# Keys and values of a linear attention as seven block products, and a softmax's divisions moved to the output's stage

## The chip, the cores and the metric

The kernel runs on one core of one Trainium2 chip. The metric is the device time of one execution in microseconds (us). TensorE (PE) multiplies, VectorE (DVE), ScalarE (ACT) and GpSimd (POOL) do elementwise work, and SyncE (SP) issues nearly every DMA. Each engine works through its own list of instructions in order; semaphores connect the lists.

## The reference

Two attention blocks read the same input of 2048 tokens by 1024 features and are mixed by a gate per token. Both have 32 heads of 32 features.

```python
g = _sigmoid((x * gate_w).sum(-1, keepdims=True))
# A: linear attention
phi = lambda t: jnp.where(t > 0, t + 1, jnp.exp(t)) + 1e-6
pq, pk = phi(q), phi(k)
kv = jnp.einsum("bhsd,bhse->bhde", pk, v)
z = jnp.einsum("bhsd->bhd", pk)
o = jnp.einsum("bhqd,bhde->bhqe", pq, kv) / (jnp.einsum("bhqd,bhd->bhq", pq, z)[..., None] + 1e-6)
# B: softmax attention
p = _softmax(jnp.einsum("bhqd,bhkd->bhqk", q, k) * (Dh ** -0.5), axis=-1)
o = jnp.einsum("bhqk,bhkd->bhqd", p, v)
# each o goes through its own wo
return g * a + (1 - g) * b
```

## The kernel before

Every float32 operand of a projection is split into a high part (a rounding copy on ACT) and a low part (the rest, a subtraction on DVE or GpSimd). One product of a 128 x 128 tile with a 128 x 512 tile is then three matmuls of 512 columns (high-high, high-low, low-high), by the helper `three` (L146 to L148) or written out (L407 to L409, L446 to L448).

The work runs in these stages:

- **Queries and keys of B, and half of its values.** Queries and keys are computed as seven block products in place of eight (Winograd's form of Strassen's product): `v_next` and `v_sums` make the four sums `t1` to `t4` of the input's blocks, `pair_ops` makes those of the weights on GpSimd, and `product` (L404) multiplies. `spill` (L329) writes the split input to DRAM (`xs`), one store per product.
- **The stream `lin`** (function `linear`, L707) then works through units of one token tile of 128 tokens and one chunk of 512 output columns, 24 matmuls each: 16 units `v` (rest of B's values), 64 units `kv` (four chunks of 256 key and 256 value columns), 32 units `q` and 32 units `o` (A's queries, and its product with `kv` and the output weights). A `kv` unit ends in `phi` on ACT (L564 to L566), one DVE instruction (L778), a running sum of the keys on GpSimd (L783, `zsum`) and eight small products in `keys` (L584). The next chunk's weights are loaded and split while the last unit of a chunk runs (`load_w`, `split_w`, L547 and L549).
- **Mixes.** During `q` and `o` units, `load_mix` (L632) brings a quarter of A's output weights into a tile, and `mix` (L649) multiplies `kv` into it. The planner lets a mix stand 8 us of its own time after the load.
- **The streams `max` and `head`** do the softmax attention of the 32 heads beside `lin`. For every head there are 64 score steps in each: `max` multiplies queries by keys (L887) and DVE takes the row maxima (L892); `head` multiplies the other way round (L1038) and ACT takes the exponential (L1042). Every four steps make one probability tile of 2048 columns, in a ring of seven. Its columns are summed over the tiles, 1536 of them on GpSimd (L1085, L1089) and 512 on DVE (`own`, L1098), and groups of five or six tiles are multiplied by the values (L1136). `finish` (L931) adds the sums over the partitions (L940); DVE then inverts them (L947), multiplies (L950), and SP stores the head's output to `oB_d`.
- **The stream `out`** multiplies B's output by its output weights, after `load_o`, `split_o` (L1191) and `gate`, and mixes in A's.

The order on PE, DVE, ACT, POOL and SP is written by a planner at the end of the kernel. It has its own clock `T` per engine and its own costs, and takes at each step the stream that can start and is furthest behind; work on DVE that may wait lies in `later` (`defer`, `fill`). The order is fixed when the program is built. `RATE_Q` and `rates` say how many `lin` matmuls stand beside one score step.

Of the kernel before, what the change touches and what calls it, by code (L numbers as in the profile page):

```python
# [18 lines left out]
P = 128  # L19
# [12 lines left out]
AHEAD = {"head": 0, "max": 6, "lin": 9, "out": 0}  # L32
# [4 lines left out]
SLACK = 0.4  # L37
WARM = 8
WO_STEP = 4
LATE = 1.0  # L40
MANUAL = {ET.PE, ET.DVE, ET.Activation, ET.SP, ET.Pool}
NMID = 14
# [3 lines left out]
def kernel(  # L46
# [53 lines left out]
    ra_d = [dram.tile([P, D], F32, name=f"ra{t}") for t in range(NT)]  # L100

# [13 lines left out]
    mh = sb.tile([NT, P], F32R, name="mh")  # L115
    ml = sb.tile([NT, P], F32R, name="ml")
# [36 lines left out]

    def use(eng, cost, *after):

        T[eng] = max(T[eng], *after, 0.0) + cost
        return T[eng] + LATENCY[eng]
# [51 lines left out]
    held = [False] * 8  # L209
    RING = [0, 1, 2, 3, 5, 6]  # L210

    def bank_at():

        times = [ended(readers[b], free[b]) for b in RING if not held[b]]
        return min((at for at in times if at is not None), default=None)

    def take():

        idle = [b for b in RING if not held[b]]
# [5 lines left out]
        held[b] = True  # L225
        return b
# [28 lines left out]
    def load_cols(w, cols, k, n):  # L255

        raw = raw_tile(n)
# [71 lines left out]
    def spill(js):  # L329

        for half in range(2):
            for jj in (1, 0):
                for i in range(TPC):
                    for p in range(2):
                        src = big[XO[PLACE[jj][half]][p]].rearrange("p (k c) -> p k c", c=C)
                        t = js[jj] * TPC + i
                        nc.sync.dma_start(xs[p][t][:, half * HK:(half + 1) * HK, :],
                                          f32(src[:, :, i * P:(i + 1) * P]))
                        yield
# [92 lines left out]
    for np_, js in enumerate(PAIRS):  # L432
        final = np_ + 1 == len(PAIRS)
        side = spill(js)
        todo = iter(())
        base = used
        for pos, k in enumerate(KORDER):
# [3 lines left out]
            for t in range(2 * TPC):  # L441
# [6 lines left out]
                nc.tensor.matmul(ps, stat[1], w[0], start=False, stop=(pos == NK - 1))  # L448
            if half:
                v_sums(i)  # L450
        used += NK
# [8 lines left out]
        for g in range(NK):  # L460
            nxt = pair_ops(g + 1) if g + 1 < NK else None
            for q, name in enumerate(PRODUCTS):
# [37 lines left out]
                next(side, None)  # L500
# [3 lines left out]
        for _ in side:  # L504
            pass
# [6 lines left out]
    chunks = [("v", c) for c in range(1, NQC)] + [("kv", c) for c in range(D // HC)]  # L512
    chunks += [(kind, c) for kind in ("q", "o") for c in range(NQC)]
    units = [(i, (t + NT // 2) % NT if chunks[i][0] == "v" else t) for i in range(len(chunks)) for t in range(NT)]
# [19 lines left out]
    def load_w(kind, c, k, n):  # L534
        if kind == "v":
            raw = load_cols(b_wqkv, vcols(c), k, n)
        elif kind == "kv":
            raw = load_cols(a_wqkv, [(D + c * HC, HC), (2 * D + c * HC, HC)], k, n)
# [11 lines left out]

    def load_xp(n):
# [5 lines left out]
        xp_ready[n % 2] = T["pe"] + 4.0  # L557
        for p, src in enumerate(oA_d if kind == "o" else xs):
# [13 lines left out]
    def keys(n, c, t, pk, va, todo):  # L572
# [3 lines left out]
        def products(b, at):  # L576
# [11 lines left out]
            def total(_):  # L588
                part = pb.rearrange("p (k d) -> p k d", d=DH)
                if t == 0:  # L590
# [10 lines left out]
    def keys_now(until):  # L601
# [4 lines left out]
        if ready:  # L606
            b = take()
# [19 lines left out]
    def load_mix():  # L627
# [5 lines left out]
        mix_here.append((a, c, T["pe"] + 8.0))  # L633
# [36 lines left out]
    z_end = [0.0, 0.0]  # L670

    def keysum(c):

        yield lambda: both(bank_at(), z_end[c % 2])
        b = take()
# [8 lines left out]
    def queries(n, c, t, pq, todo):  # L684
# [4 lines left out]
        b = take()  # L689
# [16 lines left out]

    def linear():  # L707
        extra = iter(())
        coming_w = deque()
        for n, (i, t) in enumerate(units):  # L710
            kind, c = chunks[i]
            pos = n % NT
            here_ = n < NT // 2
            follow = chunks[i + 1] if i + 1 < len(chunks) else None
            xp = xp_t[n % 2]
            yield bank_at
# [6 lines left out]
            if kind in ("q", "o") and c == 0 and t in (2, 8, NT - 2):  # L723
                yield lambda: None if mix_here else 0.0
                if t < NT - 2:
                    load_mix()
            if n < 2:
                load_head(n)
                load_v(n)
            for k in range(NK):  # L730
# [17 lines left out]
                if k == NK - 1:  # L748
# [660 lines left out]
```

## Time and profile before

| what | value |
|---|---|
| median of three runs | 2873.7 us (2872.09 to 2874.22) |
| the profiled execution | 2873.77 us, span of its instructions 2872.0 us |
| granted TensorE clock, mean | 0.996 |
| busy: VectorE | 2239.1 us |
| busy: ScalarE | 1617.8 us |
| busy: GpSimd | 1854.1 us |
| moved by DMA | 400.57 MB, mean 139 GB/s |

By the first and last starts of the lines, the stages lie in the span as follows: seven-product stage 0 to 399 us, units `v` to 504, `kv` to 1720, `q` to 2160, `o` to about 2690, output to the end. Busy time of PE includes waits inside its pipeline, so a stage is read by how many matmuls it holds per microsecond as well as by its busy share.

### The profile page before, as it was taken

The page shows a single profiled execution, that of the slowest core. Times are in us where ns is not written, and L with a number is a line of the kernel's source. Part 1 is how long each engine was busy: PE and PEld are TensorE (multiplying, and loading weights), DVE is VectorE, ACT ScalarE, POOL GpSimd, SP SyncE. Part 2 cuts the span into 40 slices and gives each one's busy share as a digit, 9 for nine tenths or more (in the row PEclk, how much of TensorE's full clock was granted, in tenths as well). Part 3 has the DMA queues.
Part 4 walks back from the last instruction along what each step waited for, and adds up shares of the span by engine and source line. Part 5 has one row for each costly group of instructions (what it writes and reads, how often), then busy time and mean ns, then how long its engine had stood idle before and what let it go on. Part 6 is the DMA issues. An engine that isn't in the chain of part 4 may idle for free.

```text
span 2872.0 us, 44436 instructions
## 1 busy us (share of the span) xinstructions
PE 2846.1 (99%) x15744; PEld 2036.8 (71%) x15744; DVE 2239.1 (78%) x3775; ACT 1617.8 (56%) x3007; POOL 1854.1 (65%) x646
## 2 busy tenths in 40 slices
PE   9999999999999999999999999899999999999999
PEld 8888888666666666666666666566766666666687
DVE  7667656788888888888888888778888888886643
ACT  5334321666666667666666666566666656656421
POOL 1212220778898889888988887578778877885000
PEclk9999999999999999999999999999999999999999
DMA  5956764332333233333332235554465344524663
GB/s 179 284 174 212 247 201 152 121 93 92 108 89 92 89 101 110 90 92 92 120 93 90 76 120 168 173 185 145 135 195 167 114 137 133 144 88 143 213 219 105
DMA packets 302498, 400.57 MB, mean 139 GB/s; under 512 B 92682, under 2 KB 185354, under 8 KB 299146
## 3 DMA queue, kind: packets, MB, share of 16 engines
q1 hardware_dynamic: 302276, 397.73, 44.8%
q8 instruction: 124, 2.03, 0.3%
q14 instruction: 98, 0.80, 0.1%
HBM read 287.57 MB, written 108.79 MB: 138 GB/s over the span
## 4 chain that ended last, share of the span: by engine, by line
PE 96%; DMA 2%; DVE 1%; ACT 0%; issue 0%; SPq 0%; ACTq 0%; DVEq 0%
PE bank L1038 16%; PE bank L887 16%; PE bank L1136 15%; PE bank L146 11%; PE bank L148 11%; PE bank L147 11%; PE bank L407 4%; PE bank L409 4%; PE bank L408 4%; PE bank L446 1%; PE bank L940 1%; PE bank L447 1%; PE bank L448 1%; DMA big<-xs 1%; PE bank L693 0%; PE bank L584 0%
## 5 line engine op out<-in xcount | busy, mean ns | idle before, releaser
L1089 POOL TENSOR_TENSOR big<-big,big 128x1536 f32<-128x1536 f32 (+1 forms) x434 | 1556.4, 3586 | 188.9 <-ACT big L1042 166.7
L892 DVE TENSOR_REDUCE mx<-bank 128x1 f32<-128x512 f32 x2048 | 1311.4, 681 | 319.6 <-PE bank L887 315.1
L1042 ACT ACTIVATE big<-bank 128x512 f32<-128x512 f32 x2048 | 1180.6, 601 | 524.8 <-PE bank L1038 455.6
L1038 PE MATMUL bank<-big,big 128*128 128x512 f32 x2048 | 810.7, 397 | 2.7 <-ACT big L1042 2.6
L887 PE MATMUL bank<-big,big 128*128 128x512 f32 x2048 | 803.6, 392 | 3.2 <-ACT mid L342 2.9
L146 PE MATMUL bank<-big,big 128*128 128x512 f32 x1408 | 552.7, 393 | 5.7 <-DMA big<-xs 3.4
L148 PE MATMUL bank<-big,big 128*128 128x512 f32 x1408 | 550.9, 391 | 1.0 <-DMA big<-oA 0.6
L147 PE MATMUL bank<-big,big 128*128 128x512 f32 x1408 | 550.6, 391 | 0.0
L1038 PEld LDWEIGHTS bank<-big,big 128*128 128x128 f32 x2048 | 384.6, 188 | 159.7 <-issue 62.0
L1136 PE MATMUL bank<-big,mid 128*32 128x512 f32 x4096 | 461.1, 595 | 0.0
L887 PEld LDWEIGHTS bank<-big,big 128*128 128x128 f32 x2048 | 385.4, 188 | 87.4 <-ACT big L1042 3.7
L1136 PEld LDWEIGHTS bank<-big,mid 128*32 128x32 f32 x4096 | 127.9, 110 | 266.2 <-issue 266.2
L146 PEld LDWEIGHTS bank<-big,big 128*128 128x128 f32 x1408 | 264.6, 188 | 71.0 <-ACT big L1042 4.3
L148 PEld LDWEIGHTS bank<-big,big 128*128 128x128 f32 x1408 | 264.8, 188 | 57.6 <-DMA big<-oA 1.0
L147 PEld LDWEIGHTS bank<-big,big 128*128 128x128 f32 x1408 | 264.5, 188 | 55.3
L1098 DVE TENSOR_TENSOR bank<-bank,big 128x512 f32<-128x512 f32 (+1 forms) x434 | 280.6, 647 | 7.8 <-ACT big L1042 6.1
L1085 POOL TENSOR_TENSOR big<-big,big 128x1536 f32<-128x1536 f32 (+1 forms) x31 | 111.6, 3601 | 253.0 <-ACT big L1042 135.5
L253 DVE TENSOR_TENSOR big<-mid,big 128x512 fp32r<-128x512 f32 x216 | 153.0, 732 | 80.5 <-ACT big L252 80.5
L386 POOL TENSOR_TENSOR mid<-mid,mid 128x512 f32<-128x512 f32 x16 | 20.6, 1291 | 276.7 <-DVE big L253 250.6
L252 ACT CAST big<-mid 128x512 fp32r<-128x512 f32 x216 | 130.2, 624 | 95.8 <-POOL mid L387 54.0
L407 PE MATMUL bank<-big,big 128*128 128x512 f32 x448 | 174.3, 389 | 0.0
L408 PE MATMUL bank<-big,big 128*128 128x512 f32 x448 | 174.3, 389 | 0.0
(103 smaller groups left out, 1981.9 us busy)
## 6 DMA issues: line engine op xcount, KB each, us to landing
big<-xs SPq DMA_DIRECT2D x208, 512.0 KB
qk<-mid SPq DMA_DIRECT2D x128, 256.0 KB
big<-oA SPq DMA_DIRECT2D x64, 512.0 KB
big<-qk SPq DMA_DIRECT2D x96, 256.0 KB
big<-qk SPq DMA_DIRECT2D x384, 64.0 KB
mid<-in_b_wqkv SPq DMA_DIRECT2D x88, 256.0 KB
xs<-big SPq DMA_DIRECT2D x64, 256.0 KB
oA<-mid SPq DMA_DIRECT2D x64, 256.0 KB
```

The costliest lines, as they stand in the source:

```text
L146: yield nc.tensor.matmul(ps, sh, mh_, start=(kt == 0), stop=False)
L147: yield nc.tensor.matmul(ps, sh, ml_, start=False, stop=False)
L148: yield nc.tensor.matmul(ps, sl, mh_, start=False, stop=(kt == NK - 1))
L407: nc.tensor.matmul(ps, sh, mh_, start=(i == 0), stop=False)
L408: nc.tensor.matmul(ps, sh, ml_, start=False, stop=False)
L887: nc.tensor.matmul(bank[b], q[:, t * P:(t + 1) * P], k[:, j * C:(j + 1) * C], start=True, stop=True)
L892: nc.vector.tensor_reduce(m[:, t, j:j + 1], bank[b], AX.X, ALU.max)
L1038: nc.tensor.matmul(bank[b], k[:, t * P:(t + 1) * P], q[:, j * C:(j + 1) * C], start=True, stop=True)
L1042: nc.scalar.activation(pr_t[i][:, j * C:(j + 1) * C], bank[b], AF.Exp, scale=SCALE)
L1089: nc.gpsimd.tensor_add(lacc[:, :qp], lacc[:, :qp], pr(t)[:, :qp])
L1098: nc.vector.tensor_add(lacc[:, qp:] if t == NT - 1 else l_b[:, :n], l_b[:, :n], src)
L1136: nc.tensor.matmul(av_b[j * DH:(j + 1) * DH, :], v[:, t, :], pr(t)[:, j * C:(j + 1) * C], start=(t == 0), stop=(t == NT - 1))
```

## The change

**Keys and values.** The 64 `kv` units become 112 products of 12 matmuls (L994): two sets of two chunks, eight pairs of token tiles, seven products each. The sums of the input's blocks are those of the first stage; they are stored there (`spill_t`, to `xt_d`) and read back. The sums of A's weights are made on GpSimd (`w_sums`, L604), the first set's during the units `v`, the second's during the products, and stored to `wt_d`. Partial results are copied out by ACT (`copy_u`, L879), some stored to `u_d` and loaded again (`load_u`); a later product starts on a bank into which ACT has copied such a result (L948), or DVE adds it (`add_u`, L886). Outputs go through `kv_out`, a stream of its own, which holds what a `kv` unit held at its end. The low parts of 56 weight tiles are made on GpSimd except those of the first eight, where there were 32 tiles, the first eight on DVE.

**Softmax sums.** For all heads but the last, `finish` copies the sums to SBUF (`l_sb`, L1285) and stores one row of each 32. After 8, 8, 8, 4 and 3 heads a packed tile is loaded, inverted in one DVE instruction (L1296) and stored to `r_d`. In the output's stage `load_r` brings the inverses of a token tile, each repeated over 32 partitions, and `scale_o` multiplies on GpSimd (L1567) ahead of `split_o`. The head's unscaled output is stored as soon as ACT has copied it.

**Planner.** `LATE` is -1.0 in place of 1.0: ahead of a row maximum the planner takes work that may wait only if it ends 1 us before the maximum can start; `own` stands in bunches in the new order, in halves where one follows another. A mix stands 25 us of planned time after its load in place of 8. `kv` has a rate of its own, 1.4, `lin` may run ahead by 40 in place of 9, and ties look at DVE's and ACT's clocks. The weights of the first chunk of `kv` are all loaded three units ahead into eight tiles in place of five.

```diff
-AHEAD = {"head": 0, "max": 6, "lin": 9, "out": 0}
+RATE_KV = 1.4
+AHEAD = {"head": 0, "max": 6, "lin": 40, "kvout": 0, "out": 0}
...
+MIX_LAND = 25.0
-LATE = 1.0
+LATE = -1.0
...
+    PHASES = ((("b11", "x"), ("b21", "x")), (("t2", "t2"),), (("t3", "t1"), ("t4", "x")), (("t1", "t3"), ("b22", "t4")))
...
+        return ([loads],
+                [lambda: add(sub, r11, r11, r12), lambda: add(plus, r12, r22, r12),
+                 lambda: add(sub, r22, r22, r11), lambda: add(sub, r21, r21, r22)],
+                [lambda n=n, r=r: store(n, r) for n, r in (("t1", r11), ("t3", r12), ("t2", r22), ("t4", r21))])
...
-        mix_here.append((a, c, T["pe"] + 8.0))
+        mix_here.append((a, c, T["pe"] + MIX_LAND))
...
+    ORDER = []
+    for m in range(NPAIR + 1):
+        ORDER += [(0, pr, q) for pr, q in ((0, m), (1, m - 1)) if 0 <= q < NPAIR]
+    ORDER += [(1, 0, q) for q in range(NPAIR)]
+    ORDER += [(2, pr, q) for q in range(NPAIR) for pr in range(2)]
+    for m in range(NPAIR + 1):
+        ORDER += [(3, pr, q) for pr, q in ((0, m), (1, m - 1)) if 0 <= q < NPAIR]
...
+        SEED = {(0, 1): (S1, lambda q: q % 4), (1, 0): (S1, lambda q: q % 4), (2, 1): (U2, lambda q: q % 2 * 2),
+                (3, 0): (U2, lambda q: q % 2 * 2), (3, 1): (W5, lambda q: q % 2 * 2)}
...
+                end = use("act", 0.6, free[b], u_at[i])
+                nc.scalar.copy(bank[b], u_tiles[i])
...
+            for k in range(HK):
...
+                for j, (x_, w) in enumerate(((sh, wh), (sh, wl), (sl, wh))):
+                    nc.tensor.matmul(bank[b], x_, w, start=(k == 0 and j == 0 and not seeded),
+                                     stop=(k == HK - 1 and j == 2), skip_group_check=seeded)
...
+                w_step()
+                if pi in last_of:
+                    split_w(None, None, slot, *loaded.popleft(), nc.gpsimd)
...
+            load_x(pi + 4)
...
                 if k == 1 and n + 1 == len(units):
+                    load_r(0, KF)
+                if k == NK - 1 and n + 1 == len(units):
                     split_o(0, slice(0, NK - 1))
-                if k == NK // 2 and n + 1 == len(units) and over["head"]:
-                    split_o(1, slice(0, NK - 1))
...
-        def store(_):
-            nc.vector.tensor_mul(avs, avs, pl)
-            for j in range(NJ):
-                nc.sync.dma_start(oB_d[j * TPC:(j + 1) * TPC, rows, g, :].rearrange("t p c -> p t c"),
-                                  avs[j * DH:(j + 1) * DH, :].rearrange("p (t c) -> p t c", c=P))
...
+        if h < H - 1:
+            need(r_left)
+            end = use("act", 0.5, end)
+            give(b, end)
+            nc.scalar.copy(l_sb, pl)
+            nc.sync.dma_start(l_d[h].rearrange("(j c) -> j c", c=C),
+                              l_sb.rearrange("(j e) c -> j e c", e=DH)[:, 0, :])
...
+                def back(_):
+                    nc.vector.reciprocal(part, part)
+                    nc.sync.dma_start(flat[1], part)
...
+            parts = 2 if after_own[0] and n == C else 1
...
+    def scale_o(n, ks):
+        rows = slice(0, P if ks == KF else LAST.start)
+        part = o_part(n, ks)[rows]
+        r = f32(blocks(xo_t[n % len(xo_t)], 1)[rows, ks])
+        nc.gpsimd.tensor_mul(part, part, r)
```

The planner's order shows three places. The first is PE in the middle of the keys and values. Before (L146 to L148 a `kv` unit, here into bank_244, with L887 and L1038 the two score matmuls):

```order
L148 MATMUL bank_244<-big_224,big_212 128x512
L146 MATMUL bank_244<-big_224,big_212 128x512
L887 MATMUL bank_249<-big_211,big_210 128x512
L147 MATMUL bank_244<-big_224,big_212 128x512
L148 MATMUL bank_244<-big_224,big_212 128x512
L1038 MATMUL bank_243<-big_208,big_209 128x512
L887 MATMUL bank_246<-big_211,big_210 128x512
L1038 MATMUL bank_245<-big_208,big_209 128x512
```

The same place of the changed kernel, where L994 is a product and L1209 and L1377 are the two score matmuls:

```order
L994 MATMUL bank_299<-big_277,big_262 128x512 x2
L1377 MATMUL bank_295<-big_260,big_261 128x512
L994 MATMUL bank_299<-big_277,big_262 128x512
L1209 MATMUL bank_297<-big_261,big_258 128x512
L1377 MATMUL bank_296<-big_260,big_261 128x512
L1209 MATMUL bank_294<-big_261,big_258 128x512
L1377 MATMUL bank_300<-big_260,big_261 128x512
L1209 MATMUL bank_295<-big_261,big_258 128x512
L994 MATMUL bank_299<-big_277,big_262 128x512
L994 MATMUL bank_297<-big_276,big_262 128x512
```

Products and scores lie interleaved as the units and scores did; bank_299 is finished and the next product begins in bank_297. Over the whole of this stage the order holds 1196 steps of each score stream before and 1012 after.

The second place is GpSimd in the same stage. Before (L1085 and L1089 sum probability tiles, L783 sums keys):

```order
L1089 TENSOR_TENSOR big_3757<-big_3757,big_3755 128x1536
L783 TENSOR_TENSOR mid_235<-mid_235,mid_232 128x256
L1089 TENSOR_TENSOR big_3757<-big_3757,big_3749 128x1536
L1089 TENSOR_TENSOR big_3757<-big_3757,big_3750 128x1536
L1089 TENSOR_TENSOR big_3757<-big_3757,big_3751 128x1536
```

After, in the last products of the first set (L1429 sums tiles, L849 sums keys, L640 makes a low part of a weight, and the sums of the second set's weights are L604 rows in between, as `big_3941<-big_3941`):

```order
L1429 TENSOR_TENSOR big_3939<-big_3939,big_3933 128x1536
L604 TENSOR_TENSOR big_3941<-big_3941 128x512
L1429 TENSOR_TENSOR big_3939<-big_3939,big_3934 128x1536
L604 TENSOR_TENSOR big_3941<-big_3941 128x512
L849 TENSOR_TENSOR mid_285<-mid_285,mid_284 128x256
L604 TENSOR_TENSOR big_3941<-big_3941 128x512
L1429 TENSOR_TENSOR big_3939<-big_3939,big_3935 128x1536
L849 TENSOR_TENSOR mid_285<-mid_285,mid_282 128x256
L1429 TENSOR_TENSOR big_3939<-big_3939,big_3936 128x1536
```

Weight sums and key sums now stand between nearly every two tile sums there.

The third place is ACT where the output begins (L252 before and L270 after split; 128x896 is seven eighths of one token tile of B's output, L822 and L1142 copy the last `o` units out, L1216 and L1599 belong to the gate). Before:

```order
L252 CAST big_21242<-mid_233 128x512
L252 CAST big_212<-big_3758 128x896
L252 CAST big_21207<-big_3753 128x896
L822 COPY mid_239<-bank_244 128x512
L1216 ACTIVATE g_sb<-g_sb 128x1
```

After:

```order
L270 CAST big_261<-mid_280 128x512
L270 CAST big_262<-big_3941 128x896
L1142 COPY mid_289<-bank_295 128x512
L270 CAST big_22034<-mid_282 128x512
L270 CAST big_22034<-mid_283 128x512
L270 CAST big_274<-big_3936 128x896
L1599 ACTIVATE g_sb<-g_sb 128x1
```

The second token tile's split stands behind the last `o` unit's copy now, and each of the two has a GpSimd multiplication ahead of it that is not in this list.

More of the change, by code (lines that the diff above doesn't have):

```diff
@@ L209, with bank_at, take @@
     held = [False] * 8
+    whole = [True] * 8
     RING = [0, 1, 2, 3, 5, 6]
-    def bank_at():
-        times = [ended(readers[b], free[b]) for b in RING if not held[b]]
+    def bank_at(seed=False):
+        times = [ended(readers[b], free[b]) for b in RING if not held[b] and (whole[b] or not seed)]
         return min((at for at in times if at is not None), default=None)
-    def take():
-        idle = [b for b in RING if not held[b]]
+    def take(seed=False, part=False, kept=False):
+        idle = [b for b in RING if not held[b] and (whole[b] or not seed)]
         times = {b: ended(readers[b], free[b]) for b in idle}
@@ L225, in take @@
         held[b] = True
+        whole[b] = whole[b] if kept else not part
         return b
@@ L670 @@
     z_end = [0.0, 0.0]
+    z_left = [[] for _ in range(2 * NSET)]
     def keysum(c):
-        yield lambda: both(bank_at(), z_end[c % 2])
-        b = take()
+        z_wait.remove(c)
+        need(z_left[c])
+        b = take(part=True)
         pz = bank[b]
@@ new lines, with u_free, load_u, copy_u @@
+    u_tiles = [mid[i] for i in (8, 9, 10, 14)]
+    u_left = [[] for _ in u_tiles]
+    u_at = [0.0] * len(u_tiles)
+    S1, U2, P7, W5 = range(4)
+    def u_free(i):
+        need(u_left[i])
+        u_left[i].clear()
+        return u_tiles[i]
+    u_what = [None] * len(u_tiles)
+    def load_u(what, pair, i):
+        nc.sync.dma_start(u_free(i), u_d[what][pair])
+        u_what[i] = what, pair
+        u_at[i] = T["pe"] + 7.0
+    def copy_u(i, b, what, pair):
+        u = u_free(i)
+        u_at[i] = use("act", 0.5, T["pe"] + LATENCY["pe"])
+        nc.scalar.copy(u, bank[b])
+        u_what[i] = what, pair
+        if what in (S1, U2, P7):
+            nc.sync.dma_start(u_d[what][pair], u)
+        return u_at[i]
@@ L890, in maxima @@
                 fill(end + LATE)
+                while True:
+                    fit = [it for it in later if it.rank <= 1 and due(it) and it.at <= T["dve"]]
+                    if not fit:
+                        break
+                    run(min(fit, key=lambda it: (it.rank, it.at)))
                 give(b, use("dve", 0.605, end))
@@ L1360 @@
             wait = max(at - T["pe"], 0.0)
-            key = (wait > 0.02, wait if wait > 0.02 else -lag)
+            busy = max(T["dve" if name == "max" else "act"] - T["pe"], 0.0) if name in ("max", "head") else 0.0
+            key = (wait > 0.02, wait + TIE * busy if wait > 0.02 else -lag, wait)
             if best is None or key < best[0]:
```

413 lines of the change are left out of this document (342 added, 71 removed).

## The prediction

> **What bounds the kernel now.** I read the page's head first, then the stretches by stage, then what PE waited for. Head and chain:
>
> ```profile
> span 2872.0 us, 44436 instructions
> PE 2846.1 (99%) x15744; PEld 2036.8 (71%) x15744; DVE 2239.1 (78%) x3775; ACT 1617.8 (56%) x3007; POOL 1854.1 (65%) x646
> PE 96%; DMA 2%; DVE 1%; ACT 0%; issue 0%; SPq 0%; ACTq 0%; DVEq 0%
> ```
>
> The chain that ended last lies on PE for 96% of the span. A busy PE need not be a full one, so I take the stretches by stage (columns: length, busy time and count of PE, weight loads, DVE, ACT, POOL, then granted clock, DMA share, GB/s):
>
> ```profile
> 0.00:399.00 399.00, 397.16 (x1743) 328.98 (x1744) 269.12 (x406) 167.46 (x294) 95.80 (x77) 1.00 0.69 214
> 399.00:504.00 105.00, 105.00 (x465) 86.70 (x464) 59.52 (x88) 13.85 (x24) 0.00 (x0) 1.00 0.59 182
> 504.00:1720.00 1216.00, 1213.06 (x7527) 826.16 (x7527) 1036.18 (x1762) 795.69 (x1535) 1055.44 (x374) 1.00 0.33 98
> 2680.00:2872.00 192.00, 185.84 (x823) 151.26 (x822) 87.25 (x204) 41.09 (x58) 0.00 (x0) 1.00 0.55 179
> ```
>
> The second row holds 512-column matmuls and nearly nothing else: 105.00 / 465 = 0.226 us each. The first gives 0.228. In the third the six matmul streams fill 1213 of 1216 us, while DVE is at 85%, POOL at 87% and ACT at 65%. So PE's matmuls set the time, and a matmul taken away is worth 0.226 to 0.228 us unless something else becomes late. What PE waited for:
>
> ```profile
> PE bank L649 <- DMA big<-in_a_wo: 7.5, 1, 7.5
> PE bank L146 <- DMA big<-xs: 3.4, 2, 2.0
> PE bank L887 <- ACT mid L342: 2.9, 1, 2.9
> PE bank L1038 <- ACT big L1042: 2.6, 1, 2.6
> PE bank L146 <- ACT big L252: 1.9, 1, 1.9
> ```
>
> These five are 18 us. Some cost more than their length:
>
> ```profile
> 506.00:516.00 10.00, 7.06 (x20) 5.55 (x20) 7.34 (x12) 6.29 (x11) 0.00 (x0) 0.66 1.00 258
> 1848.00:1854.00 6.00, 3.96 (x19) 2.99 (x18) 4.58 (x9) 4.40 (x8) 5.84 (x3) 1.00 0.67 236
> 1915.00:1925.00 10.00, 7.39 (x34) 4.23 (x36) 6.23 (x12) 5.43 (x10) 7.28 (x2) 0.83 0.69 244
> 1829.48 3.79 PE bank L649 x32
> 1789.80 1.09 PE bank L649 x32
> 1833.27 3.10 PE bank L1136 x16
> 1790.89 1.85 PE bank L1136 x16
> ```
>
> The first three are short windows around waits of 2.9, 2.0 and 2.6 us: granted clock 0.66, 1.00 and 0.83. The others are rows of the chain: the mix that came after the wait of 7.5 us took 3.79 us, its fellow at 1789 took 1.09, and the attention matmuls behind it 3.10 against 1.85. Here a wait of 2.6 us or more is followed by a stretch at half clock, one of 2.0 us isn't. The Trainium skill (TensorE: Matmul & The Clock Gate, section Why this matters for your kernels) puts the limit at about 3 us of idle time; the rows put it lower. By its limit new waits just under 3 us would cost only themselves and the sum below would be 1 to 2 us less; the measured rows decide.
>
> **The change, part by part.** The sum is made against the profiled execution, 2873.77 us, which is the median (2873.7) but for 0.1.
>
> *Matmuls.* Four chunks of 16 units of 24 matmuls, 1536, become 2 x 8 x 7 products of 12, 1344: 192 fewer. At 0.226 to 0.228 us that is 43.4 to 43.8 us, say **-43.6**. The small products, the transposes, the scores and the attention matmuls keep their counts; the scores that no longer stand beside `kv` stand beside `o`.
>
> *The mix's wait.* A mix stands 25 us behind its load in place of 8. The wait of 7.5 us, the 2.7 us by which that mix was slow (3.79 - 1.09) and 1.25 of the attention rows go: **-11.4**. What could be late next are the `xs` loads behind it (3.4 us, kept in the sum).
>
> *The first `kv` weights.* At 508 us ACT was held up by a late weight and released a bank late, 2.9 us and then a clock of 0.66. All eight weights are loaded earlier now, but DMA's share in that window is 1.00, and the input's and weights' sums now load it more. From -6 to +1; I take **-3**.
>
> *New work on ACT and DVE.*
>
> ```profile
> L1042 ACT ACTIVATE big<-bank 128x512 f32<-128x512 f32 x2048 | 1180.6, 601 | 524.8 <-PE bank L1038 455.6 <-POOL big L1089 3.2 <-issue 2.6
> L342 ACT COPY mid<-bank 128x512 f32<-128x512 f32 x32 | 18.4, 588 | 91.8 <-PE bank L148 87.5 <-PE bank L448 2.1 <-DMA v<-mid 2.1
> L947 DVE RECIPROCAL bank<-bank 128x128 f32<-128x128 f32 x128 | 123.3, 963 | 3.5 <-PE bank L940 0.4
> L950 DVE TENSOR_TENSOR mid<-mid,bank 128x512 f32<-128x512 f32 x31 | 21.3, 686 | 1.0
> L1098 DVE TENSOR_TENSOR bank<-bank,big 128x512 f32<-128x512 f32 x364 | 251.0, 689 | 5.7 <-ACT big L1042 4.5
> L1098 DVE TENSOR_TENSOR bank<-bank,big 128x256 f32<-128x256 f32 x70 | 29.7, 424 | 2.1 <-ACT big L1042 1.7
> L892 DVE TENSOR_REDUCE mx<-bank 128x1 f32<-128x512 f32 x2048 | 1311.4, 681 | 319.6 <-PE bank L887 315.1
> ```
>
> ACT gets 80 copies into banks, 64 out of them and 31 of the sums: 175 x 0.588 = 103 us. Its exponentials alone stood idle 525 us ahead of them, mostly waiting for PE, so the load is covered; what isn't covered by count is a bank's copy that PE needs next. DVE loses 124 inversions (119 us) and 31 products (21), and gets 32 additions (22) and 296 `own` in two halves, each pair 2 x 0.424 - 0.689 = 0.16 us dearer (47): some 71 us less, on an engine whose maxima waited 315 us for PE. Neither moves the end: **0**.
>
> *GpSimd.*
>
> ```profile
> L1089 POOL TENSOR_TENSOR big<-big,big 128x1536 f32<-128x1536 f32 x364 | 1272.9, 3497 | 120.4 <-ACT big L1042 100.7
> L783 POOL TENSOR_TENSOR mid<-mid,mid 128x256 f32<-128x256 f32 x60 | 44.1, 736 | 20.5 <-DVE mid L778 20.3
> L549 POOL TENSOR_TENSOR big<-big,big 128x512 fp32r<-128x512 f32 x27 | 34.7, 1295 | 3.6 <-ACT big L547 3.6
> 569.69 5.15 PE bank L1136 x48
> ```
>
> Of 1012 score steps come 253 tiles and, at 15 sums per 16, 237 sums of 3.50 us = 830; 64 key sums 47; 56 low parts (48 and the next stage's first eight) 73; 16 weight sums, priced as low parts, 21: 971 us. PE's time in the stage is 1216 less 192 + 2 x 184 matmuls (126 us) and 46 tiles of attention at 5.15 / 6 = 0.86 us (40), 1050 us. POOL goes from 87% to 92%. It isn't even: in the last quarter of the first set stand 150 score steps (35 sums), 16 key sums, 8 low parts and 8 weight sums, 123 + 12 + 10 + 10 = 155 us, against some 150 us of PE (192 + 300 matmuls, 37 tiles, switches). The ring of seven tiles takes up a lag of 5 us, but a weight's low part behind it is needed by the next product. Bounds: 0, and 25 (rival below); I take **+3**.
>
> *Loads and copies on a product's path.* No row shows a product that begins on a copied bank. Below: 0, as the copy may go out a product ahead. Above: all 80 uncovered, 80 x 0.588 = 47 us. The nearest rows are the evictions by ACT, on which PE waited twice in the whole span (2.9 and 2.6 us above), so I stay near the lower end: **+3**. SP's queue carries a few hundred more DMAs, and holds its loads back behind waits:
>
> ```profile
> SPq L559 <- PE bank L148: 162.8, 43, 16.5
> SPq L858 <- PE bank L1038: 268.7, 45, 14.8
> ```
>
> Waits of 15 us in this queue were hidden before but for 3.4 us; the new operands are asked for three products ahead, 36 matmuls with the scores between them, some 25 us. That is in the +3. In the first stage 64 stores of 256 KB are added (16.8 MB in 399 us, 42 GB/s on 214, DMA share 0.69); SP carries them between the weights' loads. From 0 to +5, I take 0.
>
> *The output's begin.* Per token tile a load of inverses and a GpSimd multiplication (3.50 x 896 / 1536 = 2.0 us, an estimate from the sums' row) now precede the split. In the steady output 2.0 to 2.5 us lie beside 48 matmuls (10.9 us) and a POOL that did nothing: 0. The first tile has no such cover: it is split at the last unit's end in place of its second product.
>
> ```profile
> L252 ACT CAST big<-big 128x896 fp32r<-128x896 f32 x2 | 1.8, 934 | 0.0
> L253 DVE TENSOR_TENSOR big<-big,big 128x896 fp32r<-128x896 f32 x2 | 2.1, 1088 | 0.1
> 2686.73 1.94 PE L940 MATMUL bank<-big,ones 128*32 128x512 f32 x16
> ```
>
> Multiplication, cast and subtraction are 4.0 us, against the last sums' matmuls of about 1.9 us; PE already waited 1.9 us there. Below: nothing more than now, 0. Above: the split 18 matmuls later (4.1), the multiplication (2.0) and half clock after a long wait (2): +8. I take the middle, **+4**.
>
> The sum: 2873.8 - 43.6 - 11.4 - 3 + 3 + 3 + 4 = **2825.8**, 1.7% faster.
>
> **The rivals.**
>
> *GpSimd sets the pace at each change of weights.* Twelve times a product's weights are split while the one before ends; if each low part stands behind a tile's sum (3.50 us) that PE has no scores to fill, 12 x 3.5 = 42 us are at stake, and I price it at 25, half covered by scores: 2850. For it: 92%, and over 100% in one quarter. Against: POOL itself waited 120 us for ACT before its sums, and the ring of tiles. The Trainium skill (GPSIMD Engine Reference, section Engine selection) would keep such subtractions on VectorE, as about twice as fast; the rows agree (1295 ns here, L1098 of the same size 689). By that rule 24 more of them are some 15 us of queue, within this rival's price.
>
> *Slower: each product waits for its start.* A product is half a unit, so its input, its copied bank and its weights must come together twice as often, through SP's one queue. Should each of 112 products wait 0.43 us on average, the 48 us are gone; a copy that is issued only once its bank is free costs its 0.59 us every time, and waits of 2.6 us or more halve the clock besides. With 0.59 us on 80 products and six such long waits of 3 us with 2 us of slow clock each: 47 + 30, 2874 + 77 - 48 = 2900. Against: copies go out one product ahead where a bank is free, and scores stand between.
>
> *More than the sum.* The `xs` waits (3.4, 2.6 and a clock of 0.83) and the short losses beside the attention matmuls go too, through the new ties and the later maxima, and the output begins without a wait: 2826 - 18 = 2808.
>
> *The mix still waits,* because SP's queue and not the planner's margin set the landing: 2837.
>
> **How the numbers follow.** The forecast, with the mix's wait gone or not, 0.62 (own range 2812 to 2840); GpSimd's pace 0.14; more than the sum 0.14; a wait at each product's start 0.10, of which some ends near no change. The range reaches from the case of more gain to GpSimd's: 2808 to 2850. It takes in the bounds of the first weights and of the output's begin. About 0.2% (5.7 us) is what a measurement of this kernel can tell from no change. Faster 0.87, the same 0.05, slower 0.08.
>
> **What would show it.** PE's matmul count 192 lower with the same 0.226 us each; no wait of the mixes on `in_a_wo`; PE's waits in the product stage a few microseconds and its clock 1.00; POOL near 92% there; a wait of 3 to 6 us before the first output matmul. Waits of PE on ACT's copies into banks, on `xt`, or on POOL's low parts by the dozen would make it wrong; so would a first stage longer than 400 us.

## The result, and the profile after

| | before | after |
|---|---|---|
| median, us (runs) | 2873.09 (2872.09 to 2874.22, 4) | 2978.15 (2973.35 to 2980.16, 4) |
| ratio, 95% interval | 1 | 1.0363 [1.0345, 1.0381] |
| span of the profiled execution, us | 2872.0 | 2976.5 |

The change makes the kernel 3.6% slower, 105 us, where 48 us of gain was forecast. The head of the page after, and its chain of work by engine (PE was 96% of it):

```profile
span 2976.5 us, 45814 instructions
PE 2855.6 (96%) x15552; PEld 2019.5 (68%) x15552; DVE 2279.2 (77%) x3953; ACT 1694.6 (57%) x3206; POOL 1964.8 (66%) x734
PE 83%; DMA 10%; DVE 2%; ACT 2%; issue 1%; SPq 1%; POOL 1%; ACTq 0%; DVEq 0%; POOLq 0%
```

The 192 matmuls are gone (15744 to 15552), and yet PE's busy time is some 10 us longer, and a tenth of the chain now lies on transfers. Where? The stretches by stage, first the output's stage of the kernel before, then four stages of the kernel after (length, busy time and count of PE, weight loads, DVE, ACT, POOL, then granted clock, DMA share, GB/s):

```profile
2692.80:2868.10 175.30, 174.87 (x768) 143.91 (x768) 76.09 (x185) 36.55 (x50) 0.00 (x0) 1.00 0.57 183
```
```profile
518.90:1587.70 1068.80, 1045.65 (x6536) 705.38 (x6536) 908.73 (x1617) 755.65 (x1518) 947.92 (x370) 1.00 0.48 138
1587.70:2024.30 436.60, 425.33 (x2280) 297.09 (x2280) 350.72 (x612) 264.73 (x508) 317.73 (x86) 0.98 0.52 161
2024.30:2710.90 686.60, 676.69 (x3766) 442.82 (x3765) 613.28 (x1045) 452.78 (x812) 544.50 (x156) 0.99 0.40 119
2710.90:2972.60 261.70, 202.09 (x768) 156.64 (x768) 76.75 (x187) 38.96 (x52) 38.26 (x31) 0.88 0.59 152
```

The output's 768 matmuls take 262 us in place of 175, at a clock of 0.88. To see the other stages I take from each stage's length 0.2266 us for every 512-column matmul of full depth (their starts lie 226 or 227 ns apart) and 0.858 us for every eight attention matmuls with 32 columns of weights, which is one probability tile or one part of the sums in `finish`. What is left is the stage's loss: waits, slow clock and small matmuls. A stage ends here where the next one's first matmul starts, so `kv` ends at 1711 us and `q` at 2150 us in the kernel before, some 10 us ahead of the last starts that the text on its stages goes by. Worked out from the trace's starts, in us, with four runs of the next part beside the two kernels (first: up to the units `v`; `o`: product and attention):

```
                 first    v     kv      q      o   output    all
before             6.7   0.2   46.2   46.4   21.8     1.3   122.6
after              6.8  15.1   78.5   45.1   37.5    87.6   270.6
e2 no loads        8.4  14.3   80.3   41.0   32.4     7.2   183.6
e3 in place        8.5  15.5   99.8   59.1   78.1     9.7   270.7
e6 rows            7.6  15.8   78.9   42.5   34.8    13.3   192.9
e9 first set       6.5   2.8   80.0   44.3   32.0    13.6   179.2
```

Loss rises by 148 us, against 43.5 us of matmuls saved (192 x 0.2266): together the 105. Of the 148 the output has 86, `kv` 32, `o` 16, `v` 15; the first stage, with its 64 extra stores, nothing.

What the output's stage waits for in the kernel after: PE for the cast of a tile, POOL (which multiplies ahead of the cast) for transfers, in us, times, longest:

```profile
PE bank L158 <- ACT big L270: 53.9, 11, 15.5
```
```profile
POOL big L1567 <- DMA big<-r: 93.6, 6, 33.0
POOL big L1567 <- DMA mid<-in_x: 55.9, 4, 14.1
POOL big L1567 <- DMA out<-big: 41.7, 3, 14.6
```

The last one to land is named `r`, `in_x` or `out`: they stand in one queue. The chain there, one token tile of it, in order of time (start, us, what):

```profile
2802.78 0.33 SPq L1523
2803.20 0.38 SPq L1535
...
2803.63 0.51 SPq L1540
2804.24 0.53 SPq L1549
...
2804.82 0.44 SPq L1549
...
2805.31 10.38 DMA big<-r
2815.75 3.50 DMA out<-big
2819.31 0.33 SPq L1523
```

A cycle of 16.5 us: the tile's seven loads of inverses are issued, land 10.4 us later, the previous output lands behind them, and only then `ra` can be loaded and the next inverses be issued. PE has 10.9 us of matmuls for a tile. And each wait costs more than itself: 59.5 us of waits in this stage bring 60.3 us at half clock, in which matmuls start 0.43 us apart. That is some 30 us more, hence about 88 us lost.

### The profile page after: what moved, and what is told of

It reads as the page before. It is cut to its first block, busy times and chain, and to the rows that moved or that the text cites. A ratio compares the mean times of both kernels' runs of the same rounds, so it can differ in the third digit from the quotient of the medians.

```text
span 2976.5 us, 45814 instructions
## 1 busy us (share of the span) xinstructions
PE 2855.6 (96%) x15552; PEld 2019.5 (68%) x15552; DVE 2279.2 (77%) x3953; ACT 1694.6 (57%) x3206; POOL 1964.8 (66%) x734
## 4 chain that ended last, share of the span: by engine, by line
PE 83%; DMA 10%; DVE 2%; ACT 2%; issue 1%; SPq 1%; POOL 1%; ACTq 0%; DVEq 0%; POOLq 0%
PE bank L1377 15%; PE bank L1481 14%; PE bank L1209 14%; PE bank L994 9%; PE bank L158 5%; PE bank L159 5%; PE bank L160 5%; DMA big<-r 4%; PE bank L437 3%; PE bank L438 3%; PE bank L439 3%; DMA out<-big 1%; DVE mx L1219 1%; PE bank L1268 1%; PE bank L475 1%
## 5 line engine op out<-in xcount | busy, mean ns | idle before, releaser
L1429 POOL TENSOR_TENSOR big<-big,big 128x1536 f32<-128x1536 f32 (+1 forms) x434 | 1557.0, 3588 | 178.1 <-ACT big L1381 157.2
L1219 DVE TENSOR_REDUCE mx<-bank 128x1 f32<-128x512 f32 x2048 | 1351.0, 688 | 289.8 <-PE bank L1209 281.7
L1381 ACT ACTIVATE big<-bank 128x512 f32<-128x512 f32 x2048 | 1163.2, 602 | 411.5 <-PE bank L1377 353.6
L1209 PE MATMUL bank<-big,big 128*128 128x512 f32 x2048 | 808.5, 396 | 20.0 <-ACT big L1381 7.9
L1377 PE MATMUL bank<-big,big 128*128 128x512 f32 x2048 | 810.4, 400 | 12.4 <-ACT big L1381 5.1
L1377 PEld LDWEIGHTS bank<-big,big 128*128 128x128 f32 x2048 | 384.0, 188 | 177.8 <-issue 49.0
L1209 PEld LDWEIGHTS bank<-big,big 128*128 128x128 f32 x2048 | 386.4, 189 | 116.8 <-DVE mx L1219 15.7
L994 PE MATMUL bank<-big,big 128*128 128x512 f32 x1344 | 457.0, 393 | 4.8 <-ACT bank L948 4.8
L158 PE MATMUL bank<-big,big 128*128 128x512 f32 x896 | 362.6, 405 | 67.8 <-ACT big L270 53.9
L160 PE MATMUL bank<-big,big 128*128 128x512 f32 x896 | 361.7, 404 | 4.5 <-DVE big L271 4.5
L159 PE MATMUL bank<-big,big 128*128 128x512 f32 x896 | 359.5, 401 | 0.6 <-DMA big<-wa 0.5
L1441 DVE TENSOR_TENSOR bank<-bank,big 128x256 f32<-128x256 f32 (+1 forms) x705 | 328.3, 466 | 30.9 <-ACT big L1381 0.4
L994 PEld LDWEIGHTS bank<-big,big 128*128 128x128 f32 x1344 | 252.8, 189 | 60.0 <-ACT bank L948 7.4
L158 PEld LDWEIGHTS bank<-big,big 128*128 128x128 f32 x896 | 174.7, 195 | 112.2 <-ACT big L270 64.9
L1567 POOL TENSOR_TENSOR big<-big,big 128x896 f32<-128x896 f32 (+1 forms) x32 | 40.3, 1281 | 271.3 <-DMA big<-r 93.6
L271 DVE TENSOR_TENSOR big<-mid,big 128x512 fp32r<-128x512 f32 x216 | 153.4, 732 | 80.8 <-ACT big L270 80.7
L160 PEld LDWEIGHTS bank<-big,big 128*128 128x128 f32 x896 | 173.8, 194 | 48.9 <-DVE big L271 11.0
L159 PEld LDWEIGHTS bank<-big,big 128*128 128x128 f32 x896 | 174.8, 195 | 38.2 <-DMA big<-wa 1.4
```

What stands on the lines that cost most here:

```text
L158: yield nc.tensor.matmul(ps, sh, mh_, start=(kt == 0), stop=False)
L159: yield nc.tensor.matmul(ps, sh, ml_, start=False, stop=False)
L160: yield nc.tensor.matmul(ps, sl, mh_, start=False, stop=(kt == NK - 1))
L271: eng.tensor_sub(lo, src, f32(hi))
L994: nc.tensor.matmul(bank[b], x_, w, start=(k == 0 and j == 0 and not seeded), stop=(k == HK - 1 and j == 2), skip_group_check=seeded)
L1209: nc.tensor.matmul(bank[b], q[:, t * P:(t + 1) * P], k[:, j * C:(j + 1) * C], start=True, stop=True)
```

## The experiments

All were timed in turn with the kernel before, whose median was 2870 to 2871.5 us in these batches.

**e1: the inverses a tile earlier.** Is it the latency of the load, or what its queue can carry?

```
+            if n == 1:
+                load_r(4, KF)
+                load_r(4, KL)
...
-                if n + 2 < NT:
-                    load_r(n + 2, KF)
-                    load_r(n + 2, KL)
+                if n + 3 < NT:
+                    load_r(n + 3, KF)
+                    load_r(n + 3, KL)
```

> The changed kernel, with a token tile's inverses loaded one tile further ahead (tile n + 3 in place of n + 2 while tile n is multiplied). Theory A, latency: an output tile waits because its inverses are asked for only one tile ahead; then the output stage falls back to some 185 us and the time to 2885 to 2915 us. Theory B, the queue: the seven loads of inverses hold SP's queue and the DMA rings for some 10 us per tile and the stores and loads behind them wait, however early they are asked for; then the time stays at 2950 us or more.

2976.76 us, ratio 1.036 [1.0342, 1.0377]: no change. A load that is asked for a tile earlier is late all the same, so it isn't latency.

**e2: no loads of inverses.** The multiplication on GpSimd stays, with what the buffer holds.

```
 def load_r(n, ks):
     need(r_left)
+    return
```

> The changed kernel without the loads of the inverses (112 DMAs); the multiplication on GpSimd stays and takes what lies in the tile, so B's output is scaled wrongly. Both theories of the output stage: it returns to 176 to 185 us and the time to 2885 to 2905 us; if GpSimd's multiplication itself were on the path (2.5 us of every tile's chain), the stage would stay above 215 us and the time above 2925 us.

2893.56 us, 1.0078 [1.0063, 1.0093]. The output's stage is 181 us and loses 7.2. So the multiplication, which the prediction had priced, costs about the 6 us by which this is above the kernel before, and the loads, which it had named and not priced, cost 85.

**e3: the divisions back in place on VectorE,** the seven products and the rest as in the kernel after.

> The changed kernel with the softmax divisions as before: DVE inverts and multiplies each head's sums in the attention stages, no loads of inverses and no GpSimd multiplication in the output. If the output stage's loss is all due to moving the divisions: output stage 176 us, time 2885 to 2905 us, still above the kernel before because the units v, the products and the units o lose some 60 us more than before. If the moved divisions had also relieved DVE where it was needed, the attention stages get longer by 10 to 30 us: 2905 to 2930 us.

2978.42 us, 1.0373 [1.0357, 1.0388]: far above either expectation. The output is as before (loss 9.7), but `kv`, `q` and `o` lose 83 us more than in e2. PE's and its weight loads' waits on VectorE's maxima point to the cause, first e3, then the kernel after (from `kv` to the end of `o`):

```profile
PE bank L1207 <- DVE mx L1217: 15.1, 33, 1.5
PE bank L1365 <- DVE mx L1217: 12.4, 17, 1.8
PEld bank L1207 <- DVE mx L1217: 52.8, 108, 1.8
PEld bank L1365 <- DVE mx L1217: 34.9, 67, 2.1
```
```profile
PE bank L1209 <- DVE mx L1219: 3.4, 9, 0.7
PE bank L1377 <- DVE mx L1219: 1.0, 2, 0.8
PEld bank L1209 <- DVE mx L1219: 15.7, 38, 1.0
PEld bank L1377 <- DVE mx L1219: 9.1, 28, 1.2
```

With seven products and the divisions in place VectorE is late in `kv`, `q` and `o` (20, 18 and 46 us over e2), and what is saved by moving the divisions there is lost again on the inverses' loads. Neither half of the change is free. The run doesn't part the seven products from the planner's new rules, which it keeps: VectorE is busy for 2392.5 us in it against 2239.1 before, and some 50 us more of its work are the halves of `own`. Seven products with divisions in place and the old rules were not tried.

**e4: the kernel before with `MIX_LAND` 25,** the planner's margin for a mix's load alone.

> The kernel before with one change: a mix stands 25 us of planned time behind its load in place of 8. If the margin is what the mix lacked, its wait of 7.5 us and the half clock behind it go: 2859 to 2865 us. If SP's queue sets the landing, or another load becomes late in its place: 2870 to 2876 us.

2870.37 us, 0.9998 [0.9989, 1.0008]. The wait of 7.5 us on `in_a_wo` is gone, stage `q` loses 29.0 in place of 46.4; but `o` loses 36.8 in place of 21.8. So the 17 us that `q` gains are lost in `o`, where PE's longest waits are now others:

```profile
PE bank L1038 <- DMA big<-ml: 6.1, 1, 6.1
PE bank L1038 <- ACT mid L822: 3.9, 1, 3.9
PE bank L903 <- ACT mid L822: 3.3, 1, 3.3
```

**e5: the weights' sums behind the head's loads.** In the kernel after, SP issues four stores of `xs` and eight weight loads ahead of the loads of `qk`, and PE waits 6.5 us for these. The queue of the kernel before, then after (start, us, line, count):

```profile
402.57 2.74 SPq L846 DMA_DIRECT2D big<-qk  x3
```
```profile
405.11 2.99 SPq L354 DMA_DIRECT2D xs<-big  x3
408.15 5.57 SPq L596 DMA_DIRECT2D mid<-in_a_wqkv  x8
413.76 1.36 SPq L1168 DMA_DIRECT2D big<-qk  x3
```

> The changed kernel with w_step() moved behind load_head and load_v in the units v, so that the weights and the stores of the sums stand behind the head's loads in SP's queue. In the changed kernel the stage of the units v lasts 119.5 us against 104.4 before, with one wait of 6.5 us of the maxima on the copy of q and k and two stretches at half clock (10.2 us). Theory (the eight weight loads that stand ahead of the head's loads in the queue make the wait): the stage falls to 106 to 112 us and the total to 2966 to 2973 us. Rival (the transfers themselves fill the DMA engines, whatever the order): the stage stays at 117 us or more, total within 3 us of 2978.

2972.24 us, 1.0357 [1.0341, 1.0373]; the stage 115.1 us in place of 119.5. That wait shrinks to 1.3 us; a second one, at 501, stays (5.9 us). The stage gains 4.4 us, less than the theory's 7.5 or more, and ends between the two expectations; the total's 6 us are within the spread of this kernel's runs (2969.7 to 2979.5).

**e6: the inverses as they are read.** Stored as `[tile, row group, group of heads, token]`, a partition's seven rows of 512 B become one run of 3584 B. Of the loads, bytes, number of transfers and readers stay; on the other side, five stores of inverses become eight.

```
-    r_d = dram.tile([H, S], F32, name="r")
+    r_d = dram.tile([NT, 4, NK, P], F32, name="r")
...
-            src = r_d.rearrange("(k r) s -> r k s", r=4)[r, ks, t * P:(t + 1) * P]
+            src = r_d[t, r, ks, :]
```

> The changed kernel with the inverses stored as they are read, [tile, row group, group of heads, token], so that one partition's seven rows of 512 B are one run of 3584 B: 224 packets for a tile in place of 992, the same bytes, the same seven transfers, still 32 partitions that read the same bytes. Theory A (the number of packets sets the 8.5 to 10.8 us of a tile's inverses): output stage 262 -> 185 to 205 us, total 2895 to 2920. Theory B (32 partitions that read the same bytes of DRAM set it, or the seven issues of 3.4 us on SP): output stage stays over 230 us, total 2945 to 2980.

2903.6 us, 1.0113 [1.0098, 1.0128]: 75 us by the layout of these rows alone. It changes the number of packets, their length and their place in DRAM together, so these three aren't parted. SP's queue, two tiles of it:

```profile
2806.60 5.03 SPq L1550 DMA_DIRECT2D big<-r  x7
2811.73 0.84 SPq L1589 DMA_DIRECT2D mid<-in_x  x2
2812.68 0.85 SPq L1627 DMA_DIRECT2D out<-big  x2
...
2818.68 5.03 SPq L1550 DMA_DIRECT2D big<-r  x7
```

and a stretch of the output's stage, after and e6 (columns as above):

```profile
2740.00:2930.00 190.00, 139.31 (x529) 107.53 (x528) 54.71 (x141) 29.31 (x39) 27.82 (x22) 0.88 0.64 173
```
```profile
2740.00:2880.00 140.00, 140.00 (x613) 115.44 (x612) 61.84 (x153) 31.73 (x41) 30.39 (x24) 0.99 0.70 224
```

The period is 12.1 us, PE is busy throughout, and the DMA engines move 224 GB/s where they moved 173 at nearly the same share of time. The seven issues take SP 5.0 us here and took 3.8 to 4.0 us in the kernel after, so they aren't what made the wait.

**e7: the inverses copied 32 times when they are stored,** so that a tile's load in the output is two transfers from bytes of their own.

> The changed kernel with the inverses copied 32 times when they are stored (31 stores of 512 rows of 512 B in the attention stages), so that a tile's load in the output stage is one transfer of 448 KB and one of 48 KB from bytes of its own, like the load of oB. Both theories of the run above expect the output stage at 180 to 200 us; the 31 stores on SP's queue cost 0 (hidden) to 60 us (2 us each, if they stand in the way of the products' loads): total 2890 to 2915 if hidden, up to 2960 if not.

2916.58 us, 1.0157 [1.014, 1.0173]. The output is the best of all with a division moved there (180 us), but `q` and `o` lose 100 us where e6's lose 77: the 31 stores are not hidden.

**e8: eight products, with the moved divisions alone,** without the inverses' loads (the output isn't scaled), to be held against e2.

> The kernel before (eight products) with the moved divisions alone: the sums copied and stored by ScalarE, reciprocals once in five groups, the multiplication on GpSimd in the output's stage, but without the loads of the inverses there (left out: the output is then not scaled by them), so it stands beside the run without those loads. VectorE is 78% busy in the kernel before. Theory A (VectorE does not set the pace with eight products, so taking 113 us of divisions from it gains nothing there): total 2865 to 2885. Theory B (the divisions delay the attention whatever the products are; with seven products they cost some 75 us in the attention's stages): 2800 to 2850.

2880.13 us, 1.0031 [1.002, 1.0043]: `kv`, `q` and `o` lose 113 us in all against 114 before, the output 9.6 against 1.3. With eight products the divisions cost nothing where they stood. Moving them is a remedy for what the seven products, with the planner's new rules, do to VectorE.

**e9: e6 with the first set's places in SP's queue mended,** `w_step()` as in e5, and the sixteen pieces of the first `kv` weights asked for in two units. In e6 twelve of them stand ahead of the `xs` of a unit in one block:

```profile
498.81 6.78 SPq L278 DMA_DIRECT2D mid<-in_a_wqkv  x12
505.68 0.85 SPq L658 DMA_DIRECT2D big<-xs  x2
```

```
-                    if pos == NT - 3:
+                    if pos == (NT - 3 if k < NK // 2 else NT - 2):
                         coming_w.append(load_w(*follow, k, LEAD_W + 1, first_raws[k]))
```

> The run with the inverses in rows (2903.6 us, stage of the units v 120.3 us with waits of 5.5 us at 416.9 on the copy of q and k and 5.2 us at 507.8 on xs, half clock for 13.7 us), with w_step() moved behind the head's loads and the sixteen pieces of the first kv weights asked for in two units in place of one. Theory (both waits are places in SP's queue): stage of the units v 106 to 110 us, total 2888 to 2895. Rival (the transfers fill the DMA engines there, and the wait moves on into the first products): total 2898 or more.

2888.67 us, 1.0063 [1.0046, 1.008]: 15 us, the stage of the units `v` back at 107.0 us with a loss of 2.8.

**e10 and e11: what makes `kv` lose 79?** e10 leaves out VectorE's additions of a kept partial sum, e11 ScalarE's copies of one into a fresh bank; both on e6.

```
e10 -        item = defer(lambda _: nc.vector.tensor_add(bank[b], bank[b], u_tiles[i]),
    +        item = defer(lambda _: None,
e11 -                nc.scalar.copy(bank[b], u_tiles[i])
```

> The run with the inverses in rows, with VectorE's 64 additions of a kept partial sum to a product's bank left out (44 us of VectorE; the planner still counts them, so the order of the rest stays; the keys and values are then wrong by these terms). Stage kv loses 78.9 us there against 46.2 in the kernel before. Theory D (VectorE is late in the products' stage because of the work that the seven products add to it): the loss falls by 15 to 30 us, total 2875 to 2890. Theory A (ScalarE's copies and the loads of partial sums on the products' path make it): the loss stays within 6 us, total 2898 to 2906.

> The run with the inverses in rows, with ScalarE's 80 copies of a kept partial sum into a fresh bank left out (48 us of ScalarE, and the wait of a product's first matmul on them; the planner still counts them; the keys and values are then wrong by these terms). Theory A (these copies on the products' path make the loss of stage kv, 78.9 us against 46.2): it falls by 15 to 30 us, total 2875 to 2890. Theory D (VectorE): it stays within 6 us, total 2898 to 2906.

e10: 2900.31 us, loss of `kv` 76.9. e11: 2892.77 us, 71.2. So the additions on VectorE cost 2 us and the 48 us of seeds (the copies into fresh banks) on ScalarE 8 us in that stage: neither theory has its 15 to 30, though the seeds are part of it. The trace of e6 counts 32 of these additions, 22.2 us in all, and not the 64 of 44 us of the expectation.

**e12: three rules of the planner as before,** on e6 (`LATE` 1.0, `TIE` 0, VectorE's own rows not in halves).

> The run with the inverses in rows, with three of the planner's rules as in the kernel before (LATE 1.0 in place of -1.0, TIE 0 in place of 0.3, VectorE's own rows of an attention sum in one addition and not in two halves). Theory P (these rules cost the waits of the attention on VectorE's additions, 25 us in 30 of them): 2875 to 2895. Theory D (they suit a VectorE that has more to do, and without them it comes later): 2905 to 2950.

2945.37 us, 1.0257 [1.0241, 1.0273]; `kv` loses 103.5, `o` 61.6. The new rules are worth 42 us with seven products; they aren't where the loss comes from.

**e13: e9 with fewer inverses at the output's begin,** behind `oB` and `ra` in the queue, four transfers for a tile in place of seven.

> The last run (2888.7 us; output stage 187.6 us against 175.3 before, with one wait of 7.9 us at 2715 behind which the clock is at half for 13.7 us) with the inverses' loads at the output's begin behind the loads of oB and ra in SP's queue, those of the fourth tile later, and four transfers for a tile in place of seven. Theory (24 transfers of inverses, 11.1 us of SP at 2694 to 2706, stand ahead of oB and ra of the third tile): output stage 177 to 182 us, total 2878 to 2884. Rival (the bytes set it): 186 us or more, total 2886 or more.

2885.77 us, 1.0057 [1.0042, 1.0072]; the output's stage 184.5 us. The wait of 7.9 us falls to 4.5. The stage lies between what the two theories asked for, and the total moved by 2.9 us, which is within the noise: not settled.

**e14 and e15: the attention's share in `kv`,** e13 with `RATE_KV` 1.2 and 1.65.

> The run above with RATE_KV 1.2 in place of 1.4: fewer of the products' matmuls for each row of the attention, so more attention in stage kv and less in stage o. Theory E (what stage kv loses over the kernel before, 80 us against 46, is ScalarE, VectorE and GpSimd being late where a row of the attention and the products' own evictions meet): its loss grows by 10 us or more, and the total is 2885 to 2910. Rival L (it is loads and copies on the products' path, whose number does not change): its loss stays within 6 us, total 2876 to 2886.

> The same with RATE_KV 1.65: less attention in stage kv and more in stage o. Theory E: the loss of stage kv falls by 10 us or more and stage o loses more; total 2870 to 2890. Rival L: the loss of stage kv stays within 6 us.

2903.02 and 2901.66 us. Stage `kv` holds 288, 250 and 213 attention tiles in e14, e13 and e15, and loses 80.8, 77.6 and 72.6 us. That is 0.11 us a tile; the kernel before, with 298 tiles, lost 46.2. By that slope, what is new in the loss doesn't go with the number of attention tiles beside the products: for the stage's loss, rival L. The totals bear out neither side as a whole: e14's lies in theory E's range and e15's above it, since `o` loses 46 and 65 in place of 35.

No version with seven products beats the kernel before. The nearest, e13, is 0.6% slower.

## Why the prediction was wrong, step by step

- **Matmuls, -43.6: right.** 192 fewer, and -43.5 at the same 0.2266 us.
- **The output, "In the steady output 2.0 to 2.5 us lie beside 48 matmuls (10.9 us) and a POOL that did nothing: 0": the step that failed,** with +86 for the whole stage. The argument holds for the multiplication, nearly (e2: +6) and was applied to a step that also had a load in it, named in the sentence before and left without a price. By the diff that load was 7 transfers of 32 partitions in 7 or 1 rows of 512 B, 992 packets a tile. The DMA share in that stage, 0.55 to 0.57 in rows of before, was the warning: a queue that is over half full needs its own sum.
- **Its begin, +4 (0 to +8): too small.** In the kernel after, the first two token tiles lose 28 of the stage's 88 us, again on the inverses. With these in rows nearly all that the stage still loses lies there: 9 to 12 us over the kernel before, with the clock (e13, e6). The wait ahead of the first output matmul is 3.9 us, within the 3 to 6 that were named.
- **The mix's wait, -11.4: failed.** "What could be late next are the `xs` loads behind it" looked at that queue only. No mix of the kernel after waits on `in_a_wo`, and yet `q` loses 45.1 us there where it lost 46.4: PE waits 3.9 us on `xs`, as was feared, and three times 1.9 to 2.5 us on ScalarE's exponentials. e4 has no gain from the margin either, since waits of 3 to 6 us on ScalarE's copy and on the rows of maxima come in `o`.
- **The first `kv` weights, -3 (-6 to +1): wrong in sign.** With the weights' sums they make the +15 of stage `v`; e9 gives back all but 3. The reason I gave for the upper end was DMA's share; it was the order in SP's queue, sixteen issues (9.0 us) ahead of one unit's `xs`.
- **Loads and copies on a product's path, +3 (0 to 47): right in kind, +32 by size.** The seeds are 8 (e11), the additions 2 (e10). One weight of a product that came late cost PE 4.9 us and then 6.8 us at half clock, some 8 in all (at 731 us in the kernel after; e9's rows below show the same wait, with 3.4 us at half clock). What makes the rest of it isn't settled by a run, but the traces say where it lies: in `kv` PE is idle for 23.1 us, against 2.9 before. ScalarE is the last to end in 16.5 us of these waits, VectorE in 5.1, GpSimd in none. Half clock takes 10.2 us in place of 6.8, which is some 2 us more, and the other 10 us or so are matmuls that stand further apart. The stage before, then two of the waits of `kv` after (the exponentials stuck behind that weight, and the seeds):

```profile
503.70:1711.20 1207.50, 1204.56 (x7490) 819.15 (x7490) 1028.82 (x1750) 789.95 (x1526) 1046.64 (x370) 1.00 0.33 99
```
```profile
PE bank L1209 <- ACT big L1381: 5.8, 2, 4.9
PE bank L994 <- ACT bank L948: 4.8, 3, 2.1
```

ScalarE, stuck behind that weight, and PE behind ScalarE, in e9 (start, us, engine, what, in brackets the wait before):

```profile
717.00 0.62 ACT L638 CAST big<-big 128x512 fp32r<-128x512 f32 x1 [5.48 <-DMA big<-wt]
...
718.16 0.50 PE L1209 MATMUL bank<-big,big 128*128 128x512 f32 x1 [4.90 <-ACT big L1382]
```

- **New work on ACT and DVE, 0: not in itself.** With eight products the divisions are free (e8), with seven they cost some 83 us in the attention's stages (e2 against e3). So "neither moves the end" holds for the kernel after only because the divisions are gone, and `o` still loses 16 more. The "some 71 us less" on VectorE was too much: its instructions took 46 us less in all, and its busy time, in which overlapping ones count once, rose from 2239.1 to 2279.2 us.
- **GpSimd, +3: right as far as it shows.** POOL is 947.92 of 1068.80 us busy in `kv`, 89%, and hardly any wait of PE names it.
- **First stage, 0: right.** DMA's share went from 0.69 to 0.82 there and its length stayed 398.3 us.
- **The rivals:** the slower one, waits at each product's start, has its mechanism in part of the 32 us of `kv`, against a price of 77. The mechanism that decided was not among them.

## What to carry to other kernels

A load that a change adds gets its own line in the sum: its packets, their size, and the queue that it stands in, even where the engine that uses it is idle. A wait that is taken away is worth what the next one leaves of it, so look at every queue that the waiting engine feeds, not at the one that it waited on. And where a change relieves one engine and loads another, price its halves apart: here the seven products with the divisions in place cost as much as the whole.

## What the runs showed of the hardware

- **Packets of 512 B.** In the output's stage after, the packets of 512 B (nine tenths of them the inverses') took 59 ns on average (2740 to 2930 us), half of them 27 ns or less; in e6, with the same bytes in runs of 3584 B, 170 ns a run, that is 24 ns for each 512 B. A tile's 992 packets went at about 100 in a microsecond, from 2806 to 2811 us with 5 to 8 of them under way at a time, where packets of 512 B in the first stage of the same kernel take 29 ns on average and reach some 670 in a microsecond. The Trainium skill (DMA: Bandwidth & Descriptors, section Specifications) gives 512 B as the size from which a transfer runs at line rate. The 75 us between the kernel after and e6 say that this did not hold for these loads. Why such a packet takes longer here isn't settled: e6 reads the same bytes into the same partitions, so that alone isn't it.
- **The clock after a short wait.** In the kernel after, every wait of PE of 2.47 us or more is followed by 3.4 us or more at half clock; of waits from 1.9 to 2.2 us three are (1.89, 2.08 and 2.12, the last one 5.7 us behind another) and two are not (2.14, 2.16). The Trainium skill (TensorE: Matmul & The Clock Gate, section Why this matters for your kernels) puts the limit at about 3 us of idle time between bursts of matmuls. The rows put it nearer 2, but no length of a wait is the limit: behind 2.76 us in e6 (at 1273 us) and 3.29 us in e4 (at 2205 us) the clock stayed full, behind 2.10 us in e9 (at 924 us) it halved. In all 17 traces the clock changes only on a grid of 3.41 us. Each of the 216 cells of this grid in which PE was idle for 1.93 us or more is followed by a cell at half clock, and of the 13932 cells at full clock in which it was idle for 1.5 us or less all but one are followed by full clock; of the 56 in between, 17 by half. So a wait that a border of the grid cuts in two can be longer without slowing the clock, and the prediction's reading (2.6 us or more yes, 2.0 us no) is no rule.
